# Attention and a gated FFN in one kernel: loads of the second batch requested earlier, and the first FFN steps in another order

## The chip, the cores and the metric

The kernel runs on one NeuronCore of a Trainium2 chip. The metric is the device time in microseconds (us) of one execution. It is the median of nine runs for the kernel before. A profiled execution gives a trace of every instruction and DMA. Its span runs from the core's first instruction to its last.

TensorE is called PE (its weight loads PEld), VectorE DVE, ScalarE ACT, GpSimd POOL and SyncE SP. L417 is line 417 of the kernel.

## What is computed

There are 8 batches, 8 heads, 576 tokens, 16 beacon tokens in front of the keys and values, and head size 64. A causal attention gives x, and a feed-forward network (FFN) with a ReLU gate works on x.

```python
k_all = concat([beacon_k, k]); v_all = concat([beacon_v, v])     # 592 keys
scores = where(causal, -1e9, q @ k_all.T / 8)                    # beacons are seen by all
a = softmax(scores)
x = (a @ v_all).transpose(0, 2, 1, 3).reshape(4608, 512)
out = (maximum(x @ w_gate, 0) * (x @ w_val)) @ w_out             # w: 512x1536, 512x1536, 1536x512
```

Inputs and the output are fp32. The kernel computes in bf16 with fp32 sums.

## The kernel before

**Attention is done in bursts.** A burst is a pair of heads, of one batch, for one of two groups of query rows: g = 0 is rows 0 to 368, g = 1 rows 368 to 576. Each batch has 4 bursts for g = 0 and then 4 for g = 1. A burst has four parts: the scores on PE (`qk`, L339), the exponential on ACT (`softmax`, L347, two slabs, each with its own score buffer of which there are two), the causal mask on DVE (`mask`, L358), and the product with v on PE (`av`, L378). The last one also divides on DVE (L386, L387) and writes x. `av` of a burst is issued in the next burst's turn.

**The FFN is done in steps.** An up step (`ffn_up`) is one block of 128 hidden columns of one token tile. It has four matmuls with the gate weights wg (L411), a ReLU on ACT (L414), four matmuls with the value weights wv (L417), and a product on DVE into hT (L425). Token tiles are 368 and 208 tokens of a batch by turns, and each has 12 up steps. hT is held in blocks of 512 tokens, so a 208-token up step of batch 0 crosses from block 0 into block 1 and takes two DVE products. A down step (`ffn_down`) makes 128 output rows. It has 12 matmuls of hT with the out weights wo (L448), a copy on ACT (L451), and an output DMA on SP (L453). `next_ffn` issues the next step of the list `ffn`, 228 steps in all.

**The order of the work is written out by hand**, and each engine runs its instructions in that order:

- A written-out start does batch 0's attention and the first FFN steps. PRE = 16 steps are issued in it. Their order is 12 up steps of 368 tokens, 2 of 208 tokens, then 2 down steps; the other 10 up steps of 208 and 2 down steps follow later (L588, L589).
- Then comes a loop over ticks 8, 9, ... A tick takes one burst, or None for a gap (GAP = 1 None after batch 1), and then as many FFN steps as a budget allows: their costs are summed and compared with what may have been spent by that tick. A step may be issued only when the x that it needs is ready, 3 ticks after the last burst that it needs.
- The steps that are left are issued after the last tick.

**Loads go through two kinds of queue.** POOL's queue (called q0, software_dynamic, in the profile) carries the loads that convert to bf16: q and k of batches 0 and 1 (`direct`, L308, into the tile cs), the weights wg and wv (L507) and wo (three DMAs of a third each, L568). SP's queue (q1, hardware_dynamic) carries v of all batches and k and q of batches 2 to 7 as fp32 into one of 6 stage buffers (L233 to L255), from where POOL casts them (L269, L282). It also carries the transposes of k and q (L296) and of x (`x_turn`, L394), and the outputs.

k and q of batches 0 and 1 are turned on PE instead (`pair_turn`, L322, with copies on DVE and ACT, L325), the beacon keys by L290. For batch 1, g = 0, a pair turn stands ahead of the scores in ticks 8, 9 and 10.

In the kernel before, the pool csb holds one buffer. c1, the k and q of batch 1, takes over the buffer of c0, batch 0's. c1 is requested behind wo, after the last pair turn of batch 0 has been issued (L611 to L613). v of batch 1 is requested on SP when 15 FFN steps are issued (FV). A small memset on DVE (L621) stands ahead of it, so that it isn't requested sooner; its place on SP's queue is behind the output DMA of the first down step. `pieces` are the loads for batches 2 to 7, 8 pieces per batch, one for each tick.

xT, the turned x, is one tile for all 4608 tokens.

```python
        FV, LEFT = len(ffn) - 15, len(ffn) - PRE
        n0 = NF + 2
        ffn[n0:2 * NF + 2] = ffn[2 * NF:2 * NF + 2] + ffn[n0:2 * NF]
...
        while len(ffn) > LEFT:
            if len(ffn) == LEFT + 1:
                bk[1].turn(V.tensor_copy)
                pair_turn(c1, 1, 0, 2, VA)
            next_ffn()
            if len(ffn) == FV:
                vl[1][0].issue(lambda ap: V.memset(ap, 0.0))
```

Of the kernel before, what the change touches and what calls it, by code (L numbers as in the profile page):

```python
# [11 lines left out]
BF16 = mybir.dt.bfloat16  # L12
# [130 lines left out]
def kernel(  # L143
# [12 lines left out]
    nc = tc.nc  # L156
    B, H, S, D = q.shape
    Nb = beacon_k.shape[2]
    P = 128
    d_model = H * D  # L160
    n_tokens = B * S
    d_ff = moe_w_gate.shape[1]
    KM, NF = d_model // P, d_ff // P
    NP = H // 2
# [4 lines left out]
    R = S // 64  # L169
# [3 lines left out]
    V, G, A, T = nc.vector, nc.gpsimd, nc.scalar, nc.tensor  # L173

    const = ctx.enter_context(tc.tile_pool(name="const", bufs=1))
    ident = const.tile([P, P], BF16, name="ident")
    ones = const.tile([P, 1], BF16, name="ones")
    xT = const.tile([P, KM, n_tokens], BF16, name="xT")
    wg = const.tile([P, KM, d_ff], BF16, name="wg")
    wv = const.tile([P, KM, d_ff], BF16, name="wv")  # L180
    wo = const.tile([P, NF, d_model], BF16, name="wo")
# [3 lines left out]
    main = ctx.enter_context(ExitStack())  # L185
# [4 lines left out]
    NSTG = 6  # L190
    stage = main.enter_context(tc.tile_pool(name="stage", bufs=NSTG))
    c16 = main.enter_context(tc.tile_pool(name="c16", bufs=4))
    csb = main.enter_context(tc.tile_pool(name="csb", bufs=1))
    xsb = main.enter_context(tc.tile_pool(name="xsb", bufs=2))
    fsb = main.enter_context(tc.tile_pool(name="fsb", bufs=2))
    osb_p = main.enter_context(tc.tile_pool(name="osb", bufs=3))
    s_ps = main.enter_context(tc.tile_pool(name="s_ps", bufs=2, space=bass.MemoryType.PSUM))
# [102 lines left out]
    def runs(src, b, p0, p1, part):  # L300
        r0, r1, s0 = PARTS[part]
        rows = src[b, 2 * p0:2 * p1, s0:s0 + (r1 - r0) * D]
        return rows.rearrange("h (p r) d -> p h (r d)", r=r1 - r0)

    def direct(c, b, p0, p1, part):
        r0, r1, _ = PARTS[part]
        for i, src in enumerate((k, q)):
            G.dma_start(c[i * D:(i + 1) * D, 2 * p0:2 * p1, r0 * D:r1 * D], runs(src, b, p0, p1, part))  # L308

    def pair_turn(c, b, p, part, cps):  # L310
        r0, r1, s0 = PARTS[part]
        n = r1 - r0
        tps = [f_ps.tile([P, n, D], BF16, name="f") for _ in range(2)]
        for r in range(r0, r1):
            for i in range(2):
                rows = slice(i * D, (i + 1) * D)
                if isinstance(c, Load):
                    flat = c.c.rearrange("p a n -> p (a n)")
                    T.transpose(tps[i][:, r - r0], flat[rows, r * P:(r + 1) * P], ident[rows, rows])  # L319
                    continue  # L320
                for a in range(2):
                    T.transpose(tps[i][a * D:(a + 1) * D, r - r0], c[rows, 2 * p + a, r * D:(r + 1) * D],  # L322
                                ident[rows, rows])
        for i in range(2):
            cps[i](kqs[b % 2][:, i, p, Nb + s0:Nb + s0 + n * D].rearrange("q (p r) -> q p r", r=n),  # L325
                   tps[i].rearrange("q r p -> q p r"))
# [4 lines left out]
    def qk(u):  # L331
        u.s, u.p = [], []
        kq = kqs[u.b % 2]
        for segs, cols, _ in SLABS[u.g]:
            s = s_ps.tile([P, 2, 512], FP32, name="s")
            for (kt, q0, n, c) in segs:
                for a in range(2):
                    rows = slice(a * D, (a + 1) * D)
                    T.matmul(s[:, a, c:c + n], kq[rows, 0, u.pi, kt * P:(kt + 1) * P],  # L339
                             kq[rows, 1, u.pi, Nb + q0:Nb + q0 + n], start=True, stop=True)  # L340
            u.s.append(s)
# [49 lines left out]
    def x_turn(u):  # L391
        for qi in QGROUPS[u.g]:
            r0, rn = QROWS[qi]
            nc.sync.dma_start_transpose(xT[:, :, u.b * S + r0:u.b * S + r0 + rn], u.x[:rn, qi, :])  # L394

    def x_turn_pair(u, cp):
        qt = QGROUPS[u.g]
        c0, c1 = QROWS[qt[0]][0], QROWS[qt[-1]][0] + QROWS[qt[-1]][1]
        tp = f_ps.tile([P, 384], BF16, name="f")
        for qi in qt:  # L400
            r0, rn = QROWS[qi]
            T.transpose(tp[:, r0 - c0:r0 - c0 + rn], u.x[:rn, qi, u.pi * P:(u.pi + 1) * P], ident[:rn, :rn])
        cp(xT[:, u.pi, u.b * S + c0:u.b * S + c1], tp[:, :c1 - c0])

    hbs = {}

    def ffn_up(m0, mn, nf):
        def go():
            g = f_ps.tile([P, 512], FP32, name="f")
            for ki in range(KM):  # L410
                T.matmul(g[:, :mn], wg[:, ki, nf * P:(nf + 1) * P], xT[:, ki, m0:m0 + mn],  # L411
                         start=(ki == 0), stop=(ki == KM - 1))
            gs = fsb.tile([P, 512], FP32, name="g")
            A.activation(gs[:, :mn], g[:, :mn], AF.Relu)  # L414
            u = f_ps.tile([P, 512], FP32, name="f")
            for ki in range(KM):
                T.matmul(u[:, :mn], wv[:, ki, nf * P:(nf + 1) * P], xT[:, ki, m0:m0 + mn],  # L417
                         start=(ki == 0), stop=(ki == KM - 1))
            c = m0
            while c < m0 + mn:  # L420
                i = c // HB
                e = min((i + 1) * HB, m0 + mn)
                if i not in hbs:
                    hbs[i] = fsb.tile([P, NF, HB], BF16, name="hT")
                V.tensor_mul(hbs[i][:, nf, c - i * HB:e - i * HB], gs[:, c - m0:e - m0], u[:, c - m0:e - m0])  # L425
                c = e
        return go
# [42 lines left out]
        V.tensor_copy(cnt, cnt_ps)  # L470

    OQ = nc.sync
    NA, PRE = 2, 16
    tiles = []
    for b in range(B):
        tiles += [(b * S, 368), (b * S + 368, 208)]
# [1 line left out]
    with tc.manual_schedule():  # L478
# [13 lines left out]
        for b in range(B):  # L492
            for p, g in [(p, g) for g in range(2) for p in range(NP)]:
                u = Burst()
# [3 lines left out]
        def start(u):  # L498
            if u.b not in xs:
                xs[u.b] = xsb.tile([P, NKT, d_model], BF16, name="x")  # L500
            u.x = xs[u.b]

        def wload(dst, src, n0, n1):
# [5 lines left out]
        def chunk(n0, n1):  # L509
            wload(wg, moe_w_gate, n0, n1)  # L510
            wload(wv, moe_w_val, n0, n1)
# [3 lines left out]
        def scores(u):  # L515
            start(u)
            qk(u)
            softmax(u)
# [6 lines left out]
        c0 = csb.tile([P, H, R * D], BF16, name="cs")  # L525
# [38 lines left out]
        vl[0][2].cast(G)  # L564
        chunk(1024, 1536)
        bk[1].cast(G)
        for j in range(0, NF, 4):
            G.dma_start(wo[:, j:j + 4], moe_w_out[j * P:(j + 4) * P].rearrange("(j p) n -> p j n", p=P))  # L568

        ffn = []  # L570
# [7 lines left out]
        def next_ffn():  # L578
            ffn.pop(0)[1]()
# [4 lines left out]
            softmax(u)  # L584
            mask(u)

        FV, LEFT = len(ffn) - 15, len(ffn) - PRE
        n0 = NF + 2  # L588
        ffn[n0:2 * NF + 2] = ffn[2 * NF:2 * NF + 2] + ffn[n0:2 * NF]  # L589

        for _ in range(NA):
# [16 lines left out]
        next_ffn()  # L608
        x_turn_pair(g1[3], V.tensor_copy)

        c1 = csb.tile([P, H, R * D], BF16, name="cs")  # L611
        direct(c1, 1, 0, 2, 2)
        direct(c1, 1, 2, NP, 2)  # L613

        while len(ffn) > LEFT:
            if len(ffn) == LEFT + 1:
                bk[1].turn(V.tensor_copy)
# [9 lines left out]
        pieces = []  # L627
        for b in range(2, B):
            kq = [Load("kq", b, t) for t in range(NKT)]
            vv = [Load("v", b, t, min(t + 2, NKT)) for t in range(0, NKT, 2)]  # L630
            pieces += [(b, x) for x in (kq[0], vv[0], kq[1], kq[2], vv[1], kq[3], kq[4], vv[2])]
        T0, GAP = 8, 1
        ticks = bursts[8:16] + [None] * GAP + bursts[16:] + [None]
        begin = {b: T0 + GAP + 8 * (b - 1) for b in range(2, B)}

# [21 lines left out]
        for s, u in enumerate(ticks, T0):  # L657
            turn = u and u.b == 1 and u.g == 0 and not u.last
            if turn:
                pair_turn(c1, 1, u.pi + 1, 2, VA)  # L660
            late = False
            if u:
                late = not turn and ffn and ready[ffn[0][2]] <= s and ffn[0][0] < 1
                start(u)
                qk(u)
                softmax(u, (0,) if late else (0, 1))
            if prev:
                av(prev)
                if prev.last:
                    x_turn(prev)  # L670
            for at, f in [j for j in jobs if j[0] == s]:
                f()
            for _ in range(1):
                if pieces and s >= begin[pieces[0][0]] - 10:
                    b, x = pieces.pop(0)
                    x.issue()
                    jobs.append((s + 2, lambda x=x: x.cast(G)))
                    if x.kind == "kq":
                        jobs.append((s + 3, lambda x=x: x.turn()))
            rest = []  # L680
            if late:
                rest = [lambda: (softmax(u, (1,)), mask(u, which=(0,))), lambda: mask(u, which=(1,))]
            elif u:
                mask(u)
            prev = u
            want += budget(s)
            while ffn and ready[ffn[0][2]] <= s and spent + ffn[0][0] / 2 <= want:
                spent += ffn[0][0]
                next_ffn()
                if rest:  # L690
                    rest.pop(0)()
            for f in rest:
                f()
# [41 lines left out]
```

## Time and profile before

| what | us |
|---|---|
| median of 9 runs (378.06 to 381.0) | 378.9 |
| the profiled execution's own time | 379.88 |
| its span | 378.2 |
| PE busy in the span | 362.0 |
| ACT, DVE, POOL busy | 204.9, 190.8, 73.1 |
| tick 8 starts (its pair turn on PE) | 48.09 |
| first 368-token up step of batch 1 | 71.64 |

The mean clock granted to PE is 0.998 of full speed. "Busy" is the time in which an engine's instructions ran, and PE's matmuls are pipelined, so that they overlap. A line of a timeline has the start, the duration, the engine, the line, the operation, the tiles written and read, and the number of instructions merged into it. In brackets stands the engine's idle time just before it, and what ended that. A line of the table by stretches has the stretch in us, its length, the busy time of the five engines (and their instructions), the clock granted to PE, the mean number of the core's DMA engines' packets under way as a share of 16, and the GB/s that they moved.

### The profile page before, as it was taken

How to read it: one execution, taken by the hardware profiler on the slowest of the kernel's cores; microseconds unless marked ns; L12 is line 12 of the kernel's file. 1: busy time of each engine (PE TensorE's matmuls, PEld its weight loads, DVE VectorE, ACT ScalarE, POOL GpSimd, SP SyncE). 2: the span in 40 equal slices, each digit the busy share in tenths (PEclk: the TensorE clock that was granted, in tenths of full speed). 3: DMA queues.
4: the chain of work that ended last, by engine and by line, in shares of the span. 5: the costliest groups of instructions: out<-in, count | busy, mean ns of one | idle time of the engine just before them, and what ended most of it. 6: DMA issues, size and time to landing. Idle time of an engine off the chain costs nothing.

```text
span 378.2 us, 9589 instructions
## 1 busy us (share of the span) xinstructions
PE 362.0 (96%) x3757; PEld 236.9 (63%) x3757; DVE 190.8 (50%) x642; ACT 204.9 (54%) x372; POOL 73.1 (19%) x94
## 2 busy tenths in 40 slices
PE   3889989999999999999999999999999999999995
PEld 2656666667746685565596647765596647765763
DVE  3766368457525674265256633565256633662230
ACT  5665366646446565455566546555466545642321
POOL 5961033211222122121303121121202000000000
PEclk9999999999999999999999999999999999999999
DMA  9999999995999797998878395779979213001202
GB/s 153 177 199 206 201 202 172 180 192 111 170 177 228 119 168 140 227 146 148 211 137 161 80 230 144 141 129 146 216 116 141 43 55 89 10 14 39 85 31 88
DMA packets 158995, 53.12 MB, mean 140 GB/s; under 512 B 146528, under 2 KB 154464, under 8 KB 158944
## 3 DMA queue, kind: packets, MB, share of 16 engines
q1 hardware_dynamic: 149840, 45.24, 63.2%
q0 software_dynamic: 8816, 6.88, 12.0%
q8 instruction: 31, 0.51, 0.6%
q10 hardware_dynamic: 288, 0.33, 0.3%
q14 instruction: 20, 0.16, 0.2%
HBM read 38.47 MB, written 9.44 MB: 127 GB/s over the span
## 4 chain that ended last, share of the span: by engine, by line
PE 89%; DMA 4%; POOL 2%; DVE 2%; issue 1%; SPq 1%; ACT 0%; ACTq 0%; DVEq 0%
PE f L417 24%; PE f L411 24%; PE f L448 23%; PE f L378 10%; PE s L339 7%; DMA wv<-in_moe_w_val_dram 2%; DMA stg<-in_v_dram 1%; DMA stg<-in_k_dram 1%; PE f L436 1%; POOL p L355 1%; DVE hT L425 1%; PE f L322 0%; DVE p L358 0%; POOL vx L269 0%; POOL wg L507 0%
## 5 line engine op out<-in xcount | busy, mean ns | idle before, releaser
L425 DVE TENSOR_TENSOR hT<-g,f 128x208 bf16<-128x208 f32 (+14 forms) x288 | 93.0, 351 | 77.7 <-PE f L417 46.8
L417 PE MATMUL f<-xT,wv 128*128 128x368 bf16 (+1 forms) x768 | 125.5, 286 | 1.4 <-DVE hT L425 0.9
L411 PE MATMUL f<-xT,wg 128*128 128x368 bf16 (+1 forms) x768 | 125.9, 286 | 0.5 <-ACT g L414 0.5
L414 ACT ACTIVATE g<-f 128x368 f32<-128x368 f32 (+1 forms) x192 | 79.1, 413 | 74.8 <-PE f L411 35.5
L347 ACT ACTIVATE p<-s 128x992 bf16<-128x992 f32 (+2 forms) x128 | 105.5, 864 | 18.2 <-PE s L339 18.1
L448 PE MATMUL f<-wo,hT 128*128 128x512 bf16 x420 | 94.2, 379 | 0.1
L417 PEld LDWEIGHTS <-wv 128*128 128x128 bf16 x768 | 71.2, 98 | 26.2 <-DVE hT L425 1.4
L411 PEld LDWEIGHTS <-wg 128*128 128x128 bf16 x768 | 69.7, 98 | 20.7 <-issue 1.5
L448 PEld LDWEIGHTS <-hT 128*128 128x128 bf16 x420 | 40.1, 98 | 44.7
L282 POOL CAST c<-stg 128x1024 bf16<-128x1024 f32 (+1 forms) x30 | 31.8, 1059 | 130.9 <-DMA stg<-in_q_dram 126.1
L451 ACT COPY ob<-f 128x512 f32<-128x512 f32 x35 | 20.5, 586 | 67.1 <-PE f L448 65.7
L386 DVE RECIPROCAL rall<-f 128x2 f32<-128x2 f32 (+1 forms) x96 | 16.7, 174 | 76.2 <-PE f L378 75.9
L378 PEld LDWEIGHTS <-p 128*128 128x128 bf16 (+2 forms) x960 | 37.0, 107 | 14.2 <-issue 12.6
L358 DVE TENSOR_TENSOR p<-p,tri 128x160 bf16<-128x160 bf16 (+1 forms) x124 | 43.3, 370 | 4.2 <-ACT p L347 3.9
L378 PE MATMUL f<-vx,p 128*128 128x65 bf16 (+2 forms) x960 | 44.1, 200 | 1.2 <-DVE p L358 0.6
L387 DVE TENSOR_TENSOR x<-f,rall 128x128 bf16<-128x128 f32 (+1 forms) x96 | 36.3, 378 | 3.4
L339 PE MATMUL s<-kq 64*128 64x208 bf16 (+4 forms) x512 | 35.4, 258 | 1.8 <-ACT p L347 1.5
L269 POOL CAST vx<-stg 128x1024 bf16<-128x1024 f32 (+2 forms) x21 | 18.9, 899 | 77.3 <-DMA stg<-in_v_dram 72.5
L339 PEld LDWEIGHTS <-kq 64*128 64x128 bf16 x512 | 16.8, 96 | 19.4 <-issue 18.2
L325 DVE COPY kq<-f 128x192 bf16<-128x192 bf16 (+2 forms) x18 | 8.6, 508 | 5.3 <-PE f L322 4.6
L319 PE MATMUL f<-ident,c 64*128 64x64 bf16 x12 | 0.5, 234 | 6.0 <-DVE c L279 6.0
L322 PEld LDWEIGHTS <-cs 64*64 64x64 bf16 x264 | 3.5, 118 | 3.2 <-issue 3.2
(50 smaller groups left out, 53.9 us busy)
## 6 DMA issues: line engine op xcount, KB each, us to landing
out_dram<-ob SPq DMA_DIRECT2D x35, 256.0 KB, 3.2
stg<-in_v_dram SPq DMA_DIRECT2D x24, 256.0 KB, 4.7
stg<-in_k_dram SPq DMA_DIRECT2D x18, 256.0 KB, 4.0
stg<-in_q_dram SPq DMA_DIRECT2D x18, 256.0 KB, 4.4
stg<-in_v_dram SPq DMA_DIRECT2D x8, 224.0 KB, 3.6
wo<-in_moe_w_out_dram POOLq DMA_DIRECT2D x3, 512.0 KB, 14.5
stg<-in_k_dram SPq DMA_DIRECT2D x6, 224.0 KB, 3.2
stg<-in_q_dram SPq DMA_DIRECT2D x6, 224.0 KB, 3.6
```

The costliest lines, as they stand in the source:

```text
L282: cp(self.c[:n], self.st[:n])
L339: T.matmul(s[:, a, c:c + n], kq[rows, 0, u.pi, kt * P:(kt + 1) * P], kq[rows, 1, u.pi, Nb + q0:Nb + q0 + n], start=True, stop=True)
L347: A.activation(p[:, :, :cols], u.s[i][:, :, :cols], AF.Exp, scale=scale)
L358: V.tensor_mul(p[:, :, :m], p[:, :, :m], tri[:, :, :m])
L378: T.matmul(o[:m, j, a, 0:D + 1], p[:kr, a, c:c + m], vs[u.b % 2][:kr, kt, 2 * u.pi + a, 0:D + 1], start=first, stop=(kt == kts[-1]), skip_ ...
L387: V.tensor_mul(u.x[:m, i0:i0 + j1 - j0, u.pi * P:(u.pi + 1) * P].rearrange("p j (a d) -> p j a d", a=2), o[:m, j0:j1, :, 0:D], r.unsqueeze ...
L411: T.matmul(g[:, :mn], wg[:, ki, nf * P:(nf + 1) * P], xT[:, ki, m0:m0 + mn], start=(ki == 0), stop=(ki == KM - 1))
L414: A.activation(gs[:, :mn], g[:, :mn], AF.Relu)
L417: T.matmul(u[:, :mn], wv[:, ki, nf * P:(nf + 1) * P], xT[:, ki, m0:m0 + mn], start=(ki == 0), stop=(ki == KM - 1))
L425: V.tensor_mul(hbs[i][:, nf, c - i * HB:e - i * HB], gs[:, c - m0:e - m0], u[:, c - m0:e - m0])
L448: T.matmul(o, hbs[i][:, nf, ms * P:(ms + 1) * P], wo[:, nf, :], start=(nf == 0), stop=(nf == NF - 1))
L451: A.copy(ob, o)
```

## The change

- csb gets a second buffer. c1, the k and q of batch 1, is requested on POOL ahead of the three DMAs of wo, and no longer waits for c0's buffer.
- v of batch 1 is requested when 10 FFN steps are issued.
- PRE is 20. The first 24 FFN steps are all of the up steps of batch 0 (12 of 368 tokens and 12 of 208), and its 4 down steps of block 0 follow them. The slice assignment at `n0 = NF + 12` changes nothing in the list.
- The turned x is a tile per batch, from a pool of 4, in place of one tile for all tokens.
- GAP is 2, so there are two gap ticks after batch 1. Loads may start 11 ticks ahead of their batch in place of 10; since the batches begin one tick later, they start in the same tick.

By the two programs' order of instructions, the kernel after has the same instructions on PE but for names and order. Its ticks 8 to 15 take these FFN steps (before | after): tick 8: 3 up of 208 | 3 up of 208; tick 9: 3 up | 1 up, 1 down; tick 10: 2 up | none; tick 11: 2 up | 1 down; ticks 12 and 13: 1 down each | 1 down each; ticks 14 and 15: 2 up of 368 each | the same. On SP, v of batch 1 and 7 DMAs of batch 2's first two pieces now stand ahead of the first output DMA. 13 up steps and 8 down steps are left after the last tick in both.

```diff
-    xT = const.tile([P, KM, n_tokens], BF16, name="xT")
...
-    csb = main.enter_context(tc.tile_pool(name="csb", bufs=1))
+    csb = main.enter_context(tc.tile_pool(name="csb", bufs=2))
     xsb = main.enter_context(tc.tile_pool(name="xsb", bufs=2))
+    xtp = main.enter_context(tc.tile_pool(name="xtp", bufs=4))
...
-            nc.sync.dma_start_transpose(xT[:, :, u.b * S + r0:u.b * S + r0 + rn], u.x[:rn, qi, :])
+            nc.sync.dma_start_transpose(xts[u.b][:, :, r0:r0 + rn], u.x[:rn, qi, :])
...
-        cp(xT[:, u.pi, u.b * S + c0:u.b * S + c1], tp[:, :c1 - c0])
+        cp(xts[u.b][:, u.pi, c0:c1], tp[:, :c1 - c0])
...
     def ffn_up(m0, mn, nf):
         def go():
+            x, c0 = xts[m0 // S], m0 % S
...
-                T.matmul(g[:, :mn], wg[:, ki, nf * P:(nf + 1) * P], xT[:, ki, m0:m0 + mn],
+                T.matmul(g[:, :mn], wg[:, ki, nf * P:(nf + 1) * P], x[:, ki, c0:c0 + mn],
...
-                T.matmul(u[:, :mn], wv[:, ki, nf * P:(nf + 1) * P], xT[:, ki, m0:m0 + mn],
+                T.matmul(u[:, :mn], wv[:, ki, nf * P:(nf + 1) * P], x[:, ki, c0:c0 + mn],
...
-    NA, PRE = 2, 16
+    NA, PRE = 2, 20
...
                 xs[u.b] = xsb.tile([P, NKT, d_model], BF16, name="x")
+                xts[u.b] = xtp.tile([P, KM, S], BF16, name="xT")
...
         bk[1].cast(G)
+        c1 = csb.tile([P, H, R * D], BF16, name="cs")
+        direct(c1, 1, 0, 2, 2)
+        direct(c1, 1, 2, NP, 2)
         for j in range(0, NF, 4):
             G.dma_start(wo[:, j:j + 4], moe_w_out[j * P:(j + 4) * P].rearrange("(j p) n -> p j n", p=P))
...
-        FV, LEFT = len(ffn) - 15, len(ffn) - PRE
-        n0 = NF + 2
+        FV, LEFT = len(ffn) - 10, len(ffn) - PRE
+        n0 = NF + 12
         ffn[n0:2 * NF + 2] = ffn[2 * NF:2 * NF + 2] + ffn[n0:2 * NF]
...
-        c1 = csb.tile([P, H, R * D], BF16, name="cs")
-        direct(c1, 1, 0, 2, 2)
-        direct(c1, 1, 2, NP, 2)
-
...
-        T0, GAP = 8, 1
+        T0, GAP = 8, 2
...
-                if pieces and s >= begin[pieces[0][0]] - 10:
+                if pieces and s >= begin[pieces[0][0]] - 11:
```

More of the change, by code (lines that the diff above doesn't have):

```diff
@@ L402, in x_turn_pair @@
             T.transpose(tp[:, r0 - c0:r0 - c0 + rn], u.x[:rn, qi, u.pi * P:(u.pi + 1) * P], ident[:rn, :rn])
-        cp(xT[:, u.pi, u.b * S + c0:u.b * S + c1], tp[:, :c1 - c0])
-    hbs = {}
+        cp(xts[u.b][:, u.pi, c0:c1], tp[:, :c1 - c0])
+    hbs, xts = {}, {}
     def ffn_up(m0, mn, nf):
         def go():
+            x, c0 = xts[m0 // S], m0 % S
             g = f_ps.tile([P, 512], FP32, name="f")
             for ki in range(KM):
-                T.matmul(g[:, :mn], wg[:, ki, nf * P:(nf + 1) * P], xT[:, ki, m0:m0 + mn],
+                T.matmul(g[:, :mn], wg[:, ki, nf * P:(nf + 1) * P], x[:, ki, c0:c0 + mn],
                          start=(ki == 0), stop=(ki == KM - 1))
```

## The prediction, made before the kernel after was run

> **What bounds the kernel now.** I read the page's totals first, then busy time by stretches, then the PE's own instructions in the stretch that is not full.
>
> ```profile
> PE 362.0 (96%) x3757; PEld 236.9 (63%) x3757; DVE 190.8 (50%) x642; ACT 204.9 (54%) x372; POOL 73.1 (19%) x94
> ```
>
> PE is busy 362.0 of 378.2 us, so only 16.2 us are to be had. Where they lie (columns: length, then busy PE, PEld, DVE, ACT, POOL, clock, DMA share, GB/s):
>
> ```profile
> 24.00:44.00 20.00, 20.00 (x235) 13.57 (x233) 12.64 (x46) 10.47 (x19) 4.84 (x8) 1.00 1.24 207
> 44.00:48.00 4.00, 3.92 (x56) 1.82 (x54) 0.95 (x2) 1.23 (x2) 0.00 (x0) 1.00 0.79 172
> 48.00:52.00 4.00, 3.52 (x73) 2.61 (x75) 2.19 (x7) 3.34 (x7) 0.00 (x1) 1.00 1.04 194
> 52.00:56.00 4.00, 3.32 (x75) 2.65 (x74) 2.98 (x8) 2.67 (x5) 3.00 (x4) 1.00 1.23 239
> 56.00:60.00 4.00, 3.61 (x80) 2.67 (x80) 3.41 (x11) 2.85 (x6) 0.59 (x1) 1.00 0.99 198
> 60.00:64.00 4.00, 3.27 (x52) 2.56 (x51) 3.62 (x13) 3.11 (x6) 1.49 (x2) 1.00 1.17 169
> 72.00:340.00 268.00, 267.85 (x2662) 175.30 (x2661) 140.19 (x488) 152.52 (x277) 43.67 (x44) 1.00 0.75 140
> ```
>
> From 72 to 340 us PE lacks 0.15 us: nothing is to be gained there. The first 24 us (9.0 us idle) and the last 18 (4.7) run the same instructions in both kernels. What the change can touch is 44 to 64 us, 2.36 us idle. DMA is as full as it gets from 24 to 44 us (207 GB/s), slack from 44 to 48. The six gaps, from PE's timeline:
>
> ```profile
> 51.01 0.52 PE L411 MATMUL f<-xT,wg 128*128 128x208 bf16 x4 [0.47 <-ACT g L414]
> 53.08 0.41 PE L378 MATMUL f<-vx,p 128*128 128x65 bf16 x8 [0.24 <-POOL vx L269]
> 53.77 0.28 PE L378 MATMUL f<-vx,p 128*128 128x65 bf16 x4 [0.28 <-POOL vx L269]
> 56.39 0.53 PE L417 MATMUL f<-xT,wv 128*128 128x208 bf16 x4 [0.56 <-DVE hT L425]
> 60.65 0.45 PE L378 MATMUL f<-vx,p 128*128 128x65 bf16 x9 [0.37 <-DVE p L358]
> 63.72 0.45 PE L378 MATMUL f<-vx,p 128*128 128x65 bf16 x9 [0.28 <-DVE p L358]
> ```
>
> v of batch 1 costs 0.52 us; ACT and DVE, loaded by narrow up steps beside attention, the rest. Busy time also hides pauses shorter than the matmul pipeline: the walk below uses starts.
>
> **What the skill says.** "DMA: Bandwidth & Descriptors", Queues, rings and completion order: each DMA engine goes round the queues that have work, a packet of several descriptors at a time, so equal shares are not promised in bytes. The trace is harsher. From 17.2 to 18.8 us batch 0's last v (SP's queue, q1) runs while weights wait in POOL's (q0); from 41 to 45 q0 is alone:
>
> ```profile
> q1 hardware_dynamic: 1336, 0.34, 110.9%
> q0 software_dynamic: 106, 0.04, 20.2%
> ...
> q0 software_dynamic: 758, 0.82, 120.7%
> ```
>
> Beside q1, q0 got 0.04 of 0.38 MB. "TensorE: Matmul & The Clock Gate", Part 1: an idle window of about 3.4 us halves PE's clock; the gaps here reach 0.56 us and the clock stays 1.00. The same page, Architectural detail: ACT and DVE take work strictly in order; the gap at 51.01 agrees (a Relu behind two exponentials).
>
> **The change, part by part.** Its four parts meet in one stretch, so I walk PE from the first up step that differs to the first up step of batch 1.
>
> *Order of FFN steps.* Steps 1 to 14 stay; up step 13 starts at 40.56 us in both. A 208-column up step takes 0.71 us (40.56 to 41.27), a down step 2.68 (41.99 to 44.67), the beacon turn and pair turn between them 0.74. Before: 2 ups, a down, the turns, a down: 40.56 + 1.43 + 2.68 + 0.74 + 2.68 = 48.09, start of tick 8. After: 7 ups, the turns, an up: 40.56 + 8 x 0.71 + 0.74 = 47.0. So tick 8 starts 1.1 us early; work of 1.1 us, net of pauses, moves into the ticks. The turns now have 0.71 us of cover plus 0.41 of the next pair turn before the scores, where they had 2.68. The copies (DVE 0.76, ACT 0.64) end some 0.9 us after the turn: I charge 0, at most 0.3.
>
> *Ticks 8 and 9.* Tick 8 keeps its three ups and the 0.47 us pause: 3.85 us as before (48.09 to 51.94), to 50.85. Tick 9 gets one up and one down for three ups. Its turn and scores take 0.9; v is long there (below), so its two pauses go; AV 0.37, up 0.71: the first down step starts at 52.83 and its later thirds, at 4 and 8 matmuls of 0.216 us, ask for the second and last third of wo at 53.7 and 54.56.
>
> *Tick 10 gets no FFN step* (the budget is spent on the down step). It leaves 1.2 us of PE work against an ACT chain that can't be shortened: after the down step (55.5) come ob copy 0.59, kq copy 0.64, exponentials of 1.00 and 0.60. The next scores wait for the first exponential's score buffer (57.8), then for the second (58.3), and AV for the mask after it. PE is free at 56.7, so 1.1 + 0.25 + 0.15 = 1.5 us idle. Such a tick isn't in the trace: bounds 0.8 (copies overlap better) and 2.2 (every hop adds).
>
> *Ticks 11 to 13* each hold a down step of 2.68 which hides softmax and masks (63 to 72 us before: no gap). From 59.0: 2.68, then 0.5 + 0.37 + 2.68, then 0.5 + 0.64 + 2.68, then 1.14 = 70.2 us, where before had 71.64. **With wo on time the change gains 1.4 us**; with the bounds of tick 10 and the turns 0.4 to 2.1.
>
> *v earlier.* Its memset moves from after step 15 to after step 10 (hT ends 38.9, memset 0.06), and SP no longer waits for the first down step's output. SP issues 6 v DMAs from 39.0 in place of 45.86; nothing on SP stops it from adding k, q and v of batch 2's first two pieces (7 DMAs), since 6 stage buffers are free. Then it stands at the first out DMA. First packets come about 2 us after issue (45.86 to 47.8), so at 41. POOL's four casts (0.6 to 1.0 us) move into its idle time before 52.
>
> *c1 ahead of wo.* Four issues of 0.62 us pass three of 0.75 on POOL, which idles from 32.2 to 52.0: issue costs nothing. The second csb buffer removes POOL's 1.3 us wait for the turns: worth nothing, q0 is backlogged to 46. c1 lands near 39 instead of 43.5 to 47.6 and is wanted at 45.5. The stall goes to what is now last: wo. Before, its thirds landed 12.7, 14.5 and 16.9 us after their issues at 24.1 to 25.6, the last at 42.5.
>
> POOL's timeline, then wo's own view:
>
> ```profile
> 24.13 2.23 POOL L568 DMA_DIRECT2D wo<-in_moe_w_out_dram  x3
> DMA to landing us min/median/max: 12.7/14.5/16.9
> ```
>
> **When wo lands.** At 41 us q0 still has what it moved from 41 to 48 before, 1.00 MB by the DMA view of that window (0.82 to 45, 0.18 after), now two thirds of wo. q1 brings 1.2 + 0.52 + 0.52 = 2.26 MB. If q1 goes first and the engines stay full, the sum is 1.00/0.206 = 4.9 us plus 2.26 at 0.263 to 0.216 MB/us (rates of v alone at 49 to 50 and 50 to 52) = 8.6 to 10.5 us: bulk done at 54.5 to 56.4, and with 1.0 for landing and for engines that lag (q0's rate fell at 45.2 and its last DMA landed at 47.6), 55.5 to 57.4 us. Asked for at 54.56: PE waits 0.9 to 2.8 us, I take 1.7. Behind it on PE is everything; on SP the out DMA, and behind that k and q of batch 2's second piece, which have over 20 us of slack (its scores began at 88).
>
> *The rest.* x held per batch adds no instruction; its buffer comes back after four batches. GAP 2 with the start moved by 1 begins loads on the same tick and bursts a tick later; the only wait that this could cover is 0.4 us of weight load for kq: credit 0.1. The steps left after the last tick are the same (13 ups, 8 downs).
>
> **Sum:** -1.4 + 1.7 - 0.1 = +0.2 us. Against the profiled execution (span 378.2, time 379.88) that is 380.1; that run lies 1.0 above the median of the nine, 378.9, so I forecast 379.1.
>
> **Rivals.** *Even shares* (0.22): q0 keeps half, 1.00 MB takes 10 us, wo is there by 52: no wait, -1.5 us, 377.4. For it: queues are served in turn; from 7 to 8 us q0 moved 0.09 MB and q1 0.10. Against it: 17.2 to 18.8. *wo later still, slower* (0.33): mixed packets lower the sum of rates to about 0.19 MB/us, 3.26 MB take 17.2 us, wo lands at 59, PE waits about 4.5 us, +3.0; 381.9 at its end, 380.9 in its middle (a wait of 3.5). It decides from a landing after 57.2, a wait over 2.6 us; a wait beyond 3.4 us may slow the clock as well. For it: q1 alone ran at 0.17 to 0.2 in places. Against it: the engines carried 0.234 MB/us in the mixed stretch. *Forecast* (0.45): 378.3 to 380.2.
>
> **Chances.** About 0.3% (1.1 us) can be told from no change. The forecast case gives 0.42 same, 0.03 slower; even shares 0.19 faster, 0.03 same; late wo 0.32 slower, 0.01 same. Faster 0.19, same 0.46, slower 0.35. The range runs from the even shares' 377.4 to 381.3, inside the late case; within the forecast alone, 378.3 to 380.2.
>
> **What would show it.** Right: no POOL gap at L378; v cast by 48; PE idle 1 to 3 us within the first down step (line 449 there) near 54.5, put down to the wo DMA; one idle of about 1.1 us before the scores of tick 11; up steps of batch 1 starting near 71.9. Wrong: wo landed before 54, or q0's bytes holding level beside v; a new wait past 72 us; tick 10 costing under 0.8.

## The result, and the profile after

The kernel after takes 383.1 us (median of 18 executions, 380.4 to 386.7), the kernel before, measured again beside it, 379.2 us (median of 55, 378.1 to 382.3). The ratio is 1.0088, with an interval from 1.0069 to 1.0106: slower by some 3.3 us. The prediction had 379.1 us and a range up to 381.3. The ratios leave out executions that were disturbed as a whole, and of the one profile below that is of such an execution, that of the kernel with all kq transposes a tick later, only the waits are read.

In the profiled executions the span goes from 378.2 to 380.7 us, so 2.5 us are to be explained. The page's totals, and its line of the clock granted to PE in 40 slices:

```profile
PE 363.1 (95%) x3757; PEld 237.5 (62%) x3757; DVE 189.1 (50%) x642; ACT 205.1 (54%) x372; POOL 73.7 (19%) x94
...
PEclk9999999999998999999999999999999999999999
```

PE is 1.1 us longer busy with the same instructions, and slice 13 (114 to 124 us) has a lower clock. Before, no slice had that. Busy time by stretches, kernel after (columns as in the prediction):

```profile
44.00:64.00 20.00, 18.64 (x317) 11.88 (x316) 13.30 (x39) 12.92 (x23) 6.10 (x7) 1.00 0.97 184
72.00:340.00 268.00, 264.78 (x2624) 172.74 (x2623) 136.57 (x473) 150.45 (x272) 44.18 (x44) 0.99 0.69 138
110.00:120.00 10.00, 6.95 (x63) 3.73 (x61) 2.32 (x8) 3.36 (x6) 1.04 (x1) 0.83 0.66 144
```

From 44 to 64 us PE is idle for 1.36 us, where it was 2.36 before. From 72 to 340 us it is idle for 3.22 us, where it was 0.15, and the last line says where: between 110 and 120 us, with the clock at 0.83 besides. PE's timeline of the kernel after shows the places:

```profile
46.59 0.48 PE L322 MATMUL f<-ident,cs 64*64 64x64 bf16 x36
...
52.40 2.75 PE L449 MATMUL f<-wo,hT 128*128 128x512 bf16 x12
...
57.26 0.78 PE L339 MATMUL s<-kq 64*128 64x128 bf16 x6 [0.81 <-ACT p L347]
...
69.77 0.80 PE L412 MATMUL f<-xT,wg 128*128 128x368 bf16 x4
...
115.38 1.39 PE L412 MATMUL f<-xT,wg 128*128 128x368 bf16 x4 [3.05 <-DMA xT<-x]
116.56 1.43 PE L418 MATMUL f<-xT,wv 128*128 128x368 bf16 x4
117.78 1.06 PE L412 MATMUL f<-xT,wg 128*128 128x368 bf16 x4
118.68 0.79 PE L418 MATMUL f<-xT,wv 128*128 128x368 bf16 x4
```

Three things are to be read here.

- The front became faster. The first 368-token up step of batch 1 starts at 69.77 us, 1.87 earlier than before (71.64). Of that, 0.6 us was gained ahead of up step 13, up to which the two kernels run the same steps: it starts at 39.95 us here and at 40.56 before. It is scatter of the start: in a second trace of the kernel after, step 13 starts at 41.03. From step 13 on the front is 1.26 us shorter (29.82 us for 31.08), in the second trace 1.5. Nothing waits for wo: the first down step (52.40) has its 12 matmuls in one group, with no idle ahead of it.
- The first up step of batch 2 (115.38) waits 3.05 us for the transposes of its x. In the second trace it is 2.46.
- After that wait the four matmuls of 368 columns take 1.39 us instead of 0.79. The two up steps last from 115.38 to 119.40, 4.02 us instead of 2.50: PE runs at half clock for about 3 us, which costs 1.5.

-1.87 + 3.05 + 1.5 = +2.7, against the 2.5 of the spans. The medians are further apart, by 3.3 by the ratio: the profiled execution of the kernel before, 379.88, lies above its median, and that of the kernel after, 382.38, below its own. Why are the transposes late? SP's timeline, kernel after:

```profile
101.38 1.88 SPq L244 DMA_DIRECT2D stg<-in_v_dram  x2
103.38 3.06 SPq L296 DMA_TRANSPOSE kq<-c  x2
106.48 0.58 SPq L254 DMA_DIRECT2D stg<-in_k_dram  x1
107.10 0.58 SPq L255 DMA_DIRECT2D stg<-in_q_dram  x1
107.78 2.25 SPq L454 DMA_DIRECT2D out_dram<-ob  x1
110.13 3.83 SPq L394 DMA_TRANSPOSE xT<-x  x3
```

and the same place in the kernel before:

```profile
102.58 2.01 SPq L244 DMA_DIRECT2D stg<-in_v_dram  x2
104.69 1.06 SPq L453 DMA_DIRECT2D out_dram<-ob  x1
105.85 4.45 SPq L394 DMA_TRANSPOSE xT<-x  x3
```

Each line ends within 0.15 us of where the next begins: SP has no pause here in either kernel. After the same v loads, the kernel after has one more pair of kq transposes (3.06 us) and one more load of k and q (0.58 + 0.58) ahead of x's transposes, and its out DMA holds SP for 2.25 us instead of 1.06. The added transposes and load belong to batch 3. Loads start in the same tick as before, and each batch's bursts one tick later. So at each point of the attention, the loads are one piece further along than they were. How late that makes x is told by DVE's line for the last x of batch 2's g = 0, kernel after:

```profile
102.36 0.56 DVE L387 TENSOR_TENSOR x<-f,rall 128x384 bf16<-128x384 f32 x1
```

and kernel before:

```profile
104.56 0.56 DVE L387 TENSOR_TENSOR x<-f,rall 128x384 bf16<-128x384 f32 x1
```

x is ready at 102.92 us, and SP reaches its transposes 7.2 us later. Before, x was ready at 105.12 us, later than that, but SP reached it after 0.7 us.

The loss is taken once. SP is full only in this part of the program: from 57 us on it has no pause over 0.5 us until 144.2 us in the kernel before and 146.7 us in the kernel after. From 200 to 340 us its pauses add up to 52 and 39 us. The kernel after's SP reaches the first x of batch 3 at 146.70 us, 12.5 us before its use at 159.22, and no later x waits.

### The profile page after: what moved, and what is told of

Same layout as the page of the kernel before. It is cut to its first block, busy times and chain, and to the rows that moved or that the text cites. A ratio compares the mean times of both kernels' runs of the same rounds, so it can differ in the third digit from the quotient of the medians.

```text
span 380.7 us, 9590 instructions
## 1 busy us (share of the span) xinstructions
PE 363.1 (95%) x3757; PEld 237.5 (62%) x3757; DVE 189.1 (50%) x642; ACT 205.1 (54%) x372; POOL 73.7 (19%) x94
## 4 chain that ended last, share of the span: by engine, by line
PE 89%; DMA 5%; ACT 2%; POOL 1%; SPq 1%; issue 0%; DVE 0%; ACTq 0%; POOLq 0%; DVEq 0%
PE f L418 25%; PE f L412 24%; PE f L449 23%; PE f L378 9%; PE s L339 7%; DMA wv<-in_moe_w_val_dram 2%; DMA stg<-in_v_dram 2%; ACT p L347 1%; DMA stg<-in_q_dram 1%; PE f L437 1%; DMA xT<-x 1%; SPq L394 1%; PE f L322 0%; POOL cs L308 0%; ACT ob L452 0%
## 5 line engine op out<-in xcount | busy, mean ns | idle before, releaser
L412 PE MATMUL f<-xT,wg 128*128 128x368 bf16 (+1 forms) x768 | 126.6, 287 | 3.6 <-DMA xT<-x 3.1
L412 PEld LDWEIGHTS <-wg 128*128 128x128 bf16 x768 | 69.8, 98 | 24.5 <-issue 5.0
L358 DVE TENSOR_TENSOR p<-p,tri 128x160 bf16<-128x160 bf16 (+1 forms) x124 | 41.2, 352 | 6.6 <-ACT p L347 6.4
```

What stands on the lines that cost most here:

```text
L358: V.tensor_mul(p[:, :, :m], p[:, :, :m], tri[:, :, :m])
L412: T.matmul(g[:, :mn], wg[:, ki, nf * P:(nf + 1) * P], x[:, ki, c0:c0 + mn], start=(ki == 0), stop=(ki == KM - 1))
```

## The experiments

Theory: SP issues its DMAs in order and is full here; what stands on it ahead of x's transposes makes x late, and the second gap tick put one more piece there. Rivals: the front's new order (wo, v or c1) costs something that only shows later; or the gap tick makes x itself late against its use.

**Loads a tick later**

```diff
-                if pieces and s >= begin[pieces[0][0]] - 11:
+                if pieces and s >= begin[pieces[0][0]] - 9:
```

> The kernel after, with the loads of batches 2 to 7 starting one tick later (9 in place of 11 ticks ahead; with two gap ticks 10 and 11 both mean tick 8). So loads stand against bursts as in the kernel before. Theory A (SP's order: with the second gap tick one more pair of k and q loads and their two transposes stand on SP ahead of the x transposes of batch 2, which then land 3 us late): no wait for xT near 115 us, the earlier part keeps its gain of 1.9 us, about 377 us. Rival B (the earlier requests and the order of the FFN steps are what costs, through a DMA backlog that reaches 110 us): the wait stays and so does 382 to 383.

Measured: 382.2 us (22 executions), 1.0057 (1.0037 to 1.0077). The wait for x is gone, as the theory says (x's transposes are issued 1.7 us after x is ready). But the time didn't come back, because a new wait stands at batch 2's first scores:

```profile
86.32 0.57 PE L339 MATMUL s<-kq 64*128 64x128 bf16 x6 [1.98 <-DMA kq<-c]
```

With its half clock behind it (86.83 to 90.89, 4.06 us for 2.5), that wait costs 3.5 us. The loads of batch 2 now come too late. There is no room on either side: a tick earlier, x is late, and a tick later, kq is. Neither expectation had this.

**One gap tick, the rest of the change kept**

```diff
-        T0, GAP = 8, 2
+        T0, GAP = 8, 1
-                if pieces and s >= begin[pieces[0][0]] - 11:
+                if pieces and s >= begin[pieces[0][0]] - 10:
```

> The kernel after with one gap tick in place of two (and 10 in place of 11): all of the change but the gap. Theory A: about 377 us, no wait for xT. Rival B: 382 to 383 with the wait.

Measured: 378.9 us, 0.9964 (0.9944 to 0.9985), and in a second measurement, told below, 379.3 us, 0.9985 (0.9969 to 1.0001). No wait for x is left. SP's timeline has the order of the kernel before again:

```profile
101.52 2.32 SPq L244 DMA_DIRECT2D stg<-in_v_dram  x2
103.94 1.07 SPq L454 DMA_DIRECT2D out_dram<-ob  x1
105.11 4.41 SPq L394 DMA_TRANSPOSE xT<-x  x3
```

So the loss belongs to the gap tick, and the front's order, v, c1 and the x per batch don't cost it.

**The kernel before with two gap ticks**

```diff
-        T0, GAP = 8, 1
+        T0, GAP = 8, 2
-                if pieces and s >= begin[pieces[0][0]] - 10:
+                if pieces and s >= begin[pieces[0][0]] - 11:
```

> The kernel before with two gap ticks (and 11 in place of 10): the gap alone. Theory A: the wait for xT appears in batch 2, 3 us and up to 2 more by a slower PE clock after it: 382 to 384. Rival B: same as before, 379.

Measured: 384.4 us (14 executions), 1.0092 (1.0060 to 1.0124). The gap alone brings the wait, in a kernel whose front is unchanged:

```profile
116.38 1.39 PE L411 MATMUL f<-xT,wg 128*128 128x368 bf16 x4 [2.81 <-DMA xT<-x]
```

The rival that blames the front is out.

**All kq transposes a tick later**

```diff
-                        jobs.append((s + 3, lambda x=x: x.turn()))
+                        jobs.append((s + 4, lambda x=x: x.turn()))
```

> The kernel after (two gap ticks) with the k and q transposes of every piece issued one tick later, so that one pair of them no longer stands on SP ahead of the x transposes of batch 2; the loads stay where they are. Theory A (SP's queue order): x transposes start some 3 us earlier, no wait for xT near 115 us; 378 to 380, what is above 378 being waits elsewhere. Rival C (x is late because the DMA engines are full, not because SP stands in line): the wait stays, 382 to 383.

Measured: 381.3 us (13 executions), 1.0038 (1.0017 to 1.0059). There is no wait for x in its profile (of which only the waits are read), and one for kq at batch 2's first scores:

```profile
91.35 0.81 PE L339 MATMUL s<-kq 64*128 64x128 bf16 x6 [2.44 <-DMA kq<-c]
```

Taking two transposes from ahead of x removes x's wait, and puts it on what was taken away.

**The wait filled with 14 matmuls of 512 columns**

```diff
+                if s == 24:
+                    fill = f_ps.tile([P, 512], FP32, name="f")
+                    for i in range(14):
+                        T.matmul(fill, wg[:, 0, 0:P], wo[:, 0, :], start=True, stop=True)
```

This adds work whose result is not used.

> The kernel after with 14 matmuls of 512 columns (3.0 us), whose result is not read, put on PE ahead of the first up step of batch 2, where PE waits 3.05 us for xT. If the wait itself slows PE's clock afterwards (0.996 in the profile, matmuls of 0.31 in place of 0.156 us between 115 and 118 us): clock back to 1.00, the wait gone from PE's idle time but not from the path, 380.4 to 381 and less scatter than 380.4 to 386.7. If the slower clock has another cause: 382 to 383 as in the kernel after.

Measured: 382.1 us (22 executions), 1.0048 (1.0027 to 1.0070), which is 0.4% or 1.5 us below the kernel after's ratio. Its profile can't show why, since the profiled execution waited elsewhere, 2.25 us at 73.58 us for batch 1's x, with half clock from the second group of matmuls on. But the mean clock is on record for every execution. Half clock for 3 us of 380 takes 0.4% from it, which leaves 0.996. With the wait filled, 19 of the 21 executions that count have a mean clock of 0.997 or more. In the kernel after, over its two measurements, 7 of 31 have. So an idle PE ahead of x is what brings the half clock in most executions, and filling it saves what the half clock cost. The time is still 1.1 us above the 380.4 to 381 that were expected: 0.6 of it is the kernel before too, which takes 379.8 us in this measurement where it took 379.2, and the rest stays open.

The profile also shows that batch 1's x has little room (in the kernel after it landed at 69.72 us and was used at 69.77).

The next three start from the kernel with one gap tick.

**One gap, c1 behind wo again**

```diff
-        c1 = csb.tile([P, H, R * D], BF16, name="cs")
-        direct(c1, 1, 0, 2, 2)
-        direct(c1, 1, 2, NP, 2)
         for j in range(0, NF, 4):
             G.dma_start(wo[:, j:j + 4], moe_w_out[j * P:(j + 4) * P].rearrange("(j p) n -> p j n", p=P))
+        c1 = csb.tile([P, H, R * D], BF16, name="cs")
+        direct(c1, 1, 0, 2, 2)
+        direct(c1, 1, 2, NP, 2)
```

> One gap tick, all of the rest of the change but c1, which is requested behind wo again. If c1's place matters: it lands from 45 to 49 us where the first pair turn asks at 45.3, PE waits 1 to 3 us there, with a slower clock after a wait over 2 us: 379 to 382 against 378.9 with c1 ahead. If it doesn't: 378.9.

Measured: 378.7 us (21 executions), 0.9994 (0.9980 to 1.0008), span 376.0. c1 lands between 43.0 and 48.8 us, and nothing waits for it. Its place is worth nothing that can be told.

**One gap, v requested at step 15 again**

```diff
-        FV, LEFT = len(ffn) - 10, len(ffn) - PRE
+        FV, LEFT = len(ffn) - 15, len(ffn) - PRE
```

> One gap tick, all of the rest of the change but v, which is requested after step 15 again (some 3.5 us later). v had landed at 48.7 to 52.9 with its first use at 51.2. If v's early request matters: PE waits up to 2 us for v near 51 us, 379 to 381. If v is carried by the engines only when q0 has drained at 48: v lands as before within 1 us, no change against 378.9.

Measured: 378.9 us, 0.9988 (0.9971 to 1.0005). v is issued 4.1 us later (from 43.12 us, against 39.02 with one gap and the early request), and its pieces behind the beacon land at 49.0 to 53.8 us, against 49.2 to 54.3. So for v itself the early request buys nothing: most of v is carried only after q0 has drained. In this trace PE waits 0.56 us for batch 1's x (70.52 us), which it doesn't in the two traces with the early request; the median shows no loss.

**One gap, the FFN steps in the old order**

```diff
-    NA, PRE = 2, 20
+    NA, PRE = 2, 16
-        n0 = NF + 12
+        n0 = NF + 2
```

> One gap tick, c1 and v requested early as in the change, but the first FFN steps in the order and number of the kernel before (first down step at 42.0 us, 16 steps ahead of tick 8). wo lands at 41.7, 44.8 and 48.2 behind c1, its last third is asked for at 43.7: PE waits about 4.5 us and loses 1.5 more by the clock, 384 to 386. If the order of the FFN steps were only a matter of ACT and DVE: 378 to 380.

Measured: 385.7 us (5 executions), 1.0171 (1.0148 to 1.0194). c1 ahead of wo makes wo late for down steps that come this early:

```profile
44.60 1.02 PE L449 MATMUL f<-wo,hT 128*128 128x512 bf16 x4 [1.46 <-DMA wo<-in_moe_w_out_dram]
48.00 1.86 PE L449 MATMUL f<-wo,hT 128*128 128x512 bf16 x4 [2.38 <-DMA wo<-in_moe_w_out_dram]
```

The new step order is what pays for c1's place.

The next two start from the kernel after again.

**One kq transpose pair behind x**

```diff
-                        jobs.append((s + 3, lambda x=x: x.turn()))
+                        jobs.append((s + (4 if s == 18 else 3), lambda x=x: x.turn()))
```

> The kernel after, with one pair of transposes moved: the turn of batch 3's second k and q tile (2 DMA transposes, 3.06 us on SP's queue at 103.38) is issued in the next tick, behind the three transposes of batch 2's x. Theory (the x transposes are late because SP's queue stands full ahead of them): they start near 107 in place of 110.1 and land near 112.2, and the first 368-column up step of batch 2 asks for them at 112.3: a wait of 0 to 0.8 us, no half clock behind it, span about 376.5, median 378.5 to 379.2, ratio 0.997 to 1.000. Rival (the gap tick makes x itself or the out DMA late, whatever stands on the queue): x transposes stay at 110, wait 3 us, median 382 to 383. Second rival (the loss moves on, as it did when every turn was a tick later): a wait for kq at batch 3's first scores, median 381 or more.

Measured: 383.1 us (11 executions), 1.0087 (1.0055 to 1.0119): no gain. PE's timeline:

```profile
114.40 0.80 PE L412 MATMUL f<-xT,wg 128*128 128x368 bf16 x4 [1.64 <-DMA xT<-x]
...
136.43 0.53 PE L412 MATMUL f<-xT,wg 128*128 128x208 bf16 x4 [2.71 <-DMA xT<-x]
```

The wait for x shrinks to 1.64 us, with no half clock. PE then waits 2.71 us for the next x of the batch, that for 208 tokens, with half clock. The loss moves on, as the second rival said, but to the next x and not to kq.

**That pair and a load behind x**

```diff
-            for _ in range(1):
+            for _ in range({21: 0, 22: 2}.get(s, 1)):
-                        jobs.append((s + 3, lambda x=x: x.turn()))
+                        jobs.append((s + (4 if s == 18 else 3), lambda x=x: x.turn()))
```

> As the run before, and the load of batch 3's fourth k and q tile (2 DMAs, 1.2 us on SP) is held back behind x's transposes too. Theory: x transposes start near 105.7 and land near 111, with no wait; about 0.5 us or less below the run before, median 378.3 to 379.0. Rival (queue length doesn't matter): 382 to 383. If the out DMA ahead of x's transposes is what stands, waiting for its copy, both runs are alike with a wait left of 1 us or more.

Measured: 385.3 us (6 executions), 1.0137 (1.0097 to 1.0177): slower still, though the interval overlaps that of the kernel after. PE doesn't wait for the first x at all, and 3.42 us for the second:

```profile
136.56 0.53 PE L412 MATMUL f<-xT,wg 128*128 128x208 bf16 x4 [3.42 <-DMA xT<-x]
```

The second expectation had the first x's wait right (none), the first hadn't (0 to 0.8 us expected, 1.64 measured), and both had the time wrong. In these runs, as in the two that moved loads or transposes by a whole tick, order on the full queue only chose who waits. Why this kernel is slower than the one before it isn't settled: its trace has 0.7 us more of wait at the second x and 1.64 us less at the first, and it starts up step 13, up to which the two are alike, 1.4 us later (41.75 us against 40.33). SP reached the second x at 132.58 us:

```profile
106.06 4.94 SPq L394 DMA_TRANSPOSE xT<-x  x3
...
132.58 2.50 SPq L394 DMA_TRANSPOSE xT<-x  x2
```

The two x's are 26.5 us apart on SP here, but on PE their uses are 19.3 apart (113.83 and 136.56 - 3.42). In the kernel before it is 20.7 us on SP (105.85 to 126.52) for 19.15 on PE (114.36 to 133.51): between these two x's SP falls behind even there, and lives on its margin until it has pauses again.

**The kernel after, and the one with one gap, on the same chip**

Both are unchanged, beside the two runs above.

> The kernel after a second time, beside the others. Ratio 1.007 to 1.011 as before, so that it stands 4 us above the kernel with one gap tick: 3.05 us of wait and 1.5 us of half clock say 4.5.

> The kernel after with one gap tick, measured a second time, now on the same chip as the kernel after and the two others. If its gain is what its trace shows (span 376.9 against 378.2 before), the ratio to before is 0.996 to 0.998; if the first measurement (0.9964) was luck of a chip, 0.998 to 1.000.

Measured: after 382.8 us, 1.0088 (1.0059 to 1.0116); one gap 379.3 us, 0.9985 (0.9969 to 1.0001). They are 3.5 us apart; the trace of this second measurement, with 2.46 us of wait and 1.5 of half clock, says 4.0. The kernel with one gap is the fastest of those tried, by 0.15 to 0.36% of the kernel before; those with c1 or v put back besides can't be told from it, and its second interval touches 1. Its profiled spans (376.9 and 376.5 against 378.2) say some 1.5 us, but these two executions lie below their medians and that of the kernel before above its own. The medians, each beside the kernel before, say 0.4 to 1.0 us.

**The outputs on POOL's queue, with two gaps and with one**

```diff
-    OQ = nc.sync
+    OQ = nc.gpsimd
```

> The kernel after with the output DMAs of the down steps requested on POOL's queue in place of SP's (but the last few). Theory (SP's queue is full from 88 to 135 us, and whatever stands on it ahead of x's transposes delays them): the out DMA at 107.78, 2.25 us, no longer stands ahead of batch 2's x; its transposes start near 108 in place of 110.1, the wait of 3.05 us shrinks to 0.5 to 1.2 with no half clock behind it, batch 2's second x doesn't wait either since two further out DMAs (1.7 us) are gone; span 377 to 378, median 379 to 380.5, ratio 0.998 to 1.003. Rival (the DMA engines, not SP's queue, are what is full, so the bytes of the outputs cost the same in POOL's queue): the wait stays at 2.5 us or more, median 382 to 383.

> The kernel with one gap tick and the outputs on POOL's queue: the control of the run before. With one gap nothing waits for x, so relief on SP should be worth nothing: 378.5 to 379.5, ratio to before 0.996 to 1.000. If outputs on POOL cost something by themselves (casts behind an output that waits for its copy), it shows here: 380 or more.

Measured: two gaps 384.0 us (6 executions), 1.0091 (1.0057 to 1.0126); one gap 379.8 us, 0.9995 (0.9979 to 1.0011). PE's wait for x with two gaps:

```profile
117.50 1.39 PE L412 MATMUL f<-xT,wg 128*128 128x368 bf16 x4 [2.06 <-DMA xT<-x]
```

and SP's transposes ahead of it:

```profile
109.99 5.50 SPq L394 DMA_TRANSPOSE xT<-x  x3
```

2.06 us lies between the two expectations, the half clock is still there, and the time is no better than the rival's 382 to 383. The profile is of the slowest of the six executions, and its PE asks for x 3.1 us later than that of the kernel after, most of it lost before 43 us. SP reaches x 4.0 us after it is ready instead of 7.2, but the three transposes then hold SP for 5.50 us instead of 3.83. Part of the relief on SP's queue is lost again in the transposes. So it isn't SP's list of entries alone: the same entry can hold SP for quite different times. That the DMA traffic decides how long is a guess that no run here tests. With one gap, 379.8 us is a little above what was expected and its ratio within it: outputs on POOL's queue cost nothing that can be told.

The first x of batch 2 in eight of these kernels (us; "asked" is PE's start less its wait, "landed" is the last of the three transposes):

| kernel | x ready | SP reaches it | landed | asked | ready to landed | ready to asked |
|---|---|---|---|---|---|---|
| before | 105.12 | 105.85 | 111.81 | 114.36 | 6.7 | 9.2 |
| after | 102.92 | 110.13 | 115.24 | 112.33 | 12.3 | 9.4 |
| before, two gaps | 104.17 | 111.15 | 116.25 | 113.57 | 12.1 | 9.4 |
| one gap | 104.02 | 105.11 | 111.03 | 113.26 | 7.0 | 9.2 |
| after, loads a tick later | 106.68 | 108.41 | 114.54 | 115.92 | 7.9 | 9.2 |
| after, one pair behind x | 103.36 | 108.27 | 114.35 | 112.76 | 11.0 | 9.4 |
| after, pair and load behind x | 104.59 | 106.06 | 112.42 | 113.83 | 7.8 | 9.2 |
| after, outputs on POOL | 106.03 | 109.99 | 117.36 | 115.44 | 11.3 | 9.4 |

The last column settles the other rival: the gap tick doesn't make x late against its use, since 9.2 to 9.4 us lie between the two in each of them. Only the time to landing differs, and PE waits wherever it is over 9.4.

## Why the prediction was wrong, by its own steps

**"The rest" failed, and it decides.** It said that two gaps with the start moved by 1 begin loads on the same tick and bursts a tick later, and "credit 0.1". The reading of the code was right; the price was not. I named only a wait that a tick of lead could remove, and didn't walk SP's queue past 72 us. That nothing was to be gained there I took to mean that nothing could be lost. Loads that run a tick earlier against the bursts stand ahead of x's transposes, which the bursts make. The margin could be read in the trace of before: x's transposes landed at 111.81 us and were used at 114.36, 2.55 us. One piece costs SP there 2.5 to 3.5 us for two kq transposes and 1.16 for the load, 3.7 to 4.7 in all. The estimate from those, 1.1 to 2.1 us of wait, would have given this term the right sign. It would still have been too small: the out DMA ahead of x also held SP 1.2 us longer. In place of -0.1 stand 3.05 us of wait and 1.5 us of half clock.

**"If q1 goes first and the engines stay full" failed.** It put wo's landing at 55.5 to 57.4 us and charged 1.7. wo's thirds landed at 41.65, 44.78 and 48.19 us, and were asked for from 52.40: no wait. So the 1.7 us charged here didn't come, while 4.5 came under the term that was credited; in the sum these two errors partly hide each other. The DMA view of the kernel after from 43 to 45 us, in which both queues have packets:

```profile
q0 software_dynamic: 308, 0.31, 91.0%
q1 hardware_dynamic: 310, 0.08, 29.8%
```

308 packets against 310: in this stretch the queues go one for one. q0's packets are of 1 KB and q1's of 256 bytes, so q0 moves four times the bytes. The Trainium skill's "DMA: Bandwidth & Descriptors", Queues, rings and completion order, has the engines take turns between the queues at the grain of packets; the equal counts agree with that, though they don't show how many packets make a turn. I set that page aside for the stretch from 17.2 to 18.8 us of the kernel before, where q0 moved little. Perhaps q0 had little ready to move then; the trace doesn't show what is ready. Nor is the 207 GB/s from 24 to 44 us as full as it gets: the prediction's own table has 239 from 52 to 56.

**"Order of FFN steps" held.** Tick 8 starts at 46.59 us (forecast 47.0), and the first down step at 52.40 (52.83). Step 13, though, does not start at 40.56 us in both, as the prediction read, but at 39.95 here; from it to tick 8 are 6.6 us (forecast 6.4). The pause ahead of L412 stayed, as forecast (0.44 us at 49.47). The turns' smaller cover cost nothing.

**Tick 10** costs 0.81 us of idle in one piece before its successor's scores (57.26), where 1.5 was taken and 0.8 was the lower bound. Ticks 11 to 13, from the down step at 58.37 to the up step at 69.77, take 11.4 us (forecast 11.2) with no gap.

**"With wo on time the change gains 1.4 us"**: that term was right. From step 13 to the first up step of batch 1, 1.26 us were gained in the first trace of the kernel after and 1.51 in the second; the 1.87 us at 69.77 us hold 0.6 of an earlier start. This part of the sum is the rival of even shares, and the kernel with one gap is that rival without the gap's loss: 378.9 and 379.3 us, 0.15 to 0.36% under the kernel before, where that rival had 377.4, or 0.40% under.

**"v earlier" failed without harm.** I had v cast by 48 us. It landed from 48.7 to 52.9: SP stood for almost 5 us at one issue (39.85, the next at 44.72), and from 43 to 45 us q1 got one small packet for each large one of q0. AV at 51.24 us didn't wait.

**"c1 ahead of wo"**: its cost of nothing was right as far as c1 itself goes (landed by 39.2, no wait). That the stall goes to wo was right only with the old step order (1.46 + 2.38 us, shown above).

**The rival that ended slower** had the sign, not the mechanism: it had PE wait for wo. In its one remark on what lies past 72 us, "a new wait past 72 us" under what would show it wrong, the prediction named what then happened, with no price and no chance for it.

## What to carry to other kernels

When a change shifts loads against compute, list each in-order DMA queue for the whole steady part before and after, and compare the extra entries ahead of each late-made transfer with the margin between its landing and its use in the trace of before. In a stretch where a queue has no pause between its entries, there is no room to reorder it: in each of the four kernels here that moved loads or transposes on it, the wait moved to another transfer. An engine that is 96% busy hides a full queue, as long as nothing waits for it.

## What the runs showed of the hardware that I had not expected

- Half clock came after shorter idle times than I had charged. The Trainium skill's "TensorE: Matmul & The Clock Gate", Part 1, gives an idle window of about 3.4 us; here waits of 1.98, 2.06, 2.25, 2.46, 2.71, 2.81, 3.05 and 3.42 us were each followed by matmuls at half clock (1.39 us for 0.79, or 0.90 for 0.52), after three of them with up to 1.1 us at full clock in between. Waits of 0.81 and 1.64 us in the same kernels were not. The half clock lasted about 3 us, so the wait of 1.98 us cost 3.5.
- Two queues that both had packets took them one for one from 43 to 45 us (308 and 310; 313 and 317 with one gap), though one's were four times as large.
- A DMA transpose of x held SP for 1.2 us at best and for up to 2.85 (one of the three that took 5.50 with outputs on POOL). A plain load of 256 KB of k or q took mostly 0.58. Of the 12.6 us of SP's time from 101.38 to 113.96 us in the kernel after, transposes are 6.9.
